# A three-row matmul given all 128 rows through a masked copy, and a store moved to ScalarE's queue

## The chip, the core and the metric

The kernel runs on one core of a Trainium2 chip. The metric is the device time of one execution in microseconds (us); lower is better. Three runs of the kernel before took 2999.73, 3000.49 and 3001.02 us, so its median is 3000.49 us.

## What is computed

Three layers stand behind each other; `x` is 4 batches of 3072 samples by 256.

```
X = fft over 256 of fft over 3072 of x; keep the real part
h = relu(X @ w_in); u, v = halves of h (512 each)
v_n = (v - mean) / sqrt(var + 1e-6)              per sample
v_s = w_spatial (3072x3072) @ v_n + b_spatial
y = (u * v_s) @ w_out
out = (sigmoid(y @ w_gate) * (y @ w_val)) @ w_out2
```

All is in float32; a product is three matmuls of rounded parts (high times high, high times low, low times high), which the kernel calls `mm3`.

## The kernel before

**Stage 1 (about 72 to 362 us)** does the Fourier transform and the first product, for four batches b = 0 to 3. In a batch the outputs come in four *units* (3, 2, 0, 1 in that order), each of 7 or 8 *blocks*: `v_block(m)` makes 128 samples by 512 columns of v, `u_block(fb)` 128 columns of u by 384 samples. A block first runs `mm3` and then one matmul of its own, line 585 in a v block and line 617 in a u block. That one adds the sample at half the rate in the model dimension (index 128 of 256), which the 128 other rows can't hold. It contracts three rows only: `nt` holds, for each unit, three rows of each batch at partitions 32b to 32b+2, zeros elsewhere being of no meaning to it, and `own = slice(32 * b, 32 * b + 3)` picks the batch. ScalarE then copies the sum to `ev` or `eu` (lines 592, 619). Two blocks later comes the block's second half (`second`: `mm3` again, then ScalarE's copy or ReLU at lines 599 and 625 and VectorE's mirror at line 577), and one block later its `rest` (a ReLU on ScalarE, line 605, statistics on VectorE, line 607). A list of steps, one a block, says which other work is written between blocks: folds of the next batch's input (GpSimd, lines 353 to 371), transforms (`fft`, TensorE, the tile `psf`), the taking of transforms into parts `ph`, `pl` (lines 420, 421), normalisation (`ln1` to `norms`, lines 638 to 660) and stores. Every engine runs its instructions in the order in which they are written.

The transforms of units 0 and 1 come out of one pair of sums: ScalarE copies the first half-sum to `even` (line 854), and VectorE makes the other unit's values from it into `value` (line 859). For the last batch the two transforms start at steps 10 and 11 of its 29 (`END0`).

**Stage 2 (about 362 to 1885 us)** is the product with `w_spatial`, by a scheme of seven products in place of eight over 2x2 blocks. It has 42 *leaves* (2 pairs of batches, 7 products, 3 column ranges), each of six steps `kp` of 24 matmuls of 128x512 into four PSUM banks. Operands are loaded five steps ahead by SyncE's queue into 7 staging tiles `st` (line 735), added (line 744, GpSimd for v, VectorE for w), rounded by ScalarE (line 748) and their rest taken by VectorE (line 751). During the next leaf, VectorE takes the four banks (lines 966 to 985), and in the leaves that complete an output also the low parts `gl` (line 993); then two halves of `second` multiply with `w_out` (12 matmuls each), ScalarE copies each half to `x2` (line 1032), and after the other half SyncE's queue stores `x2` (line 1034). There are 24 such stores.

**Stage 3 (about 1885 to 2995 us)** is the last layer, and the change does not touch it.

Of the kernel before, what the change touches and what calls it, by code (L numbers as in the profile page):

```python
# [9 lines left out]
F32 = mybir.dt.float32  # L10
F32R = mybir.dt.float32r
# [3 lines left out]
AF = mybir.ActivationFunctionType  # L15
ALU = mybir.AluOpType
# [3 lines left out]
B, S, D = 4, 3072, 256  # L20
# [4 lines left out]
P = 128  # L25
H = 384
R3 = H + 2
# [105 lines left out]


def _masks():
    m = np.zeros((P, 4), np.float32)
    for b in range(B):
        m[32 * b + 2, 0] = -1.0
        m[32 * b + 1, 1] = -1.0
    m[64:68, 2] = -1.0  # L140
    return m
# [96 lines left out]
def tile_kernel(ctx: ExitStack, tc: tile.TileContext, t: dict, out: bass.AP):  # L238
# [10 lines left out]
    def f(ap):  # L249
        return ap.bitcast(F32)  # L250
# [63 lines left out]
    ps_f = pool(ps0, "ps_f", 2, space=PSUM)  # L314
    ps_w = pool(ps0, "ps_w", 6, space=PSUM)

    masks = keep.tile([P, 4], F32, name="masks")
    gc = [keep.tile([P, 2, DFF], F32R, name=f"g{n}") for n in "hl"]
    g3 = keep.tile([P, DFF], F32R, name="g3")
    nts = [keep.tile([P, R3 if unit == 3 else H], F32R, name=f"nt{unit}") for unit in range(4)]  # L320
# [225 lines left out]
    def take_nyquist(ps, n, unit):  # L546
        nc.scalar.copy(nts[unit], ps[:, :n])
        nc.vector.scalar_tensor_tensor(
            out=nts[unit], in0=f(nts[unit]), scalar=masks[:, 0:1], in1=ps[:, :n], op0=ALU.mult, op1=ALU.add
        )  # L550

    for unit in (3, 2):
        take_nyquist(*fft(fold_n, B, unit, 0), unit)
    s0.close()
    stp = pool(r0, "stp", 2, "right")
    vp = pool(r0, "vp", 13, "right")
# [2 lines left out]
    def unit_blocks(pq, b, unit):  # L559

        (ph, pl), (qh, ql) = pq

        queue = nc.gpsimd if b == B - 1 and unit < 2 else nc.sync
        nt = nts[unit]
        vsl = slice(DH, DFF)

        own = slice(32 * b, 32 * b + 3)
        nb = 7 if unit == 3 else 6
        tiles = {}
        stats = stp.tile([P, 7, 6], F32, name="stats")  # L570
        mv = stp.tile([P, 7, 2], F32, name="mv")
        ve, sd, y, nm = (stp.tile([P, 7], F32, name=n) for n in ("ve", "sd", "y", "nm"))

        def mirror(to, part, ps):
            nc.vector.scalar_tensor_tensor(out=to, in0=part, scalar=2.0, in1=ps, op0=ALU.mult, op1=ALU.subtract)

        def v_block(m):

            w0 = m * P if m < 3 else R3 - P
            win = slice(w0, w0 + P)
            ps = ps_w.tile([P, 512], F32, tag="pa", name="psv")
            mm3(ps, (ph[:, win], pl[:, win]), (gc[0][:, 0, vsl], gc[1][:, 0, vsl]), True, False)
            nc.tensor.matmul(out=ps, lhsT=nt[own, win], rhs=g3[own, vsl], start=False, stop=True)  # L585
            if m == 3:
                tv = vp.tile([P, DH], F32, tag="tv", name="tv")
                nc.scalar.activation(tv, ps, AF.Relu)
                tiles[6] = tv
                return lambda: lambda: nc.vector.bn_stats(stats[:, 6, :], tv)  # L590
            ev = stp.tile([P, DH], F32, tag="e", name="ev", bufs=4)
            nc.scalar.copy(ev, ps)

            def second():
                weights = (gc[0][:, 1, vsl], gc[1][:, 1, vsl])
                mm3(ps, (qh[:, win], ql[:, win]), weights, False, True, skip_group_check=True)
                for sg in range(2):
                    tiles[sg * 3 + m] = vp.tile([P, DH], F32, tag="tv", name="tv")
                nc.scalar.activation(tiles[m], ps, AF.Relu)
                mirror(tiles[3 + m], ev, ps)  # L600
                return rest

            def rest():
                tv = tiles[3 + m]
                nc.scalar.activation(tv, tv, AF.Relu)
                for sg in range(2):
                    nc.vector.bn_stats(stats[:, sg * 3 + m, :], tiles[sg * 3 + m])

            return second

        def u_block(fb):

            fsl = slice(fb * P, fb * P + P)
            n = R3 if unit == 3 else H
            ps = ps_w.tile([P, 512], F32, tag="pa", name="psu")
            mm3(ps[:, :n], (gc[0][:, 0, fsl], gc[1][:, 0, fsl]), (ph[:, :n], pl[:, :n]), True, False)
            nc.tensor.matmul(out=ps[:, :n], lhsT=g3[own, fsl], rhs=nt[own, :n], start=False, stop=True)
            eu = stp.tile([P, R3], F32, tag="e", name="eu", bufs=4)
            nc.scalar.copy(eu[:, :n], ps[:, :n])

            def second():
                weights = (gc[0][:, 1, fsl], gc[1][:, 1, fsl])
                mm3(ps[:, :H], weights, (qh[:, :H], ql[:, :H]), False, True, skip_group_check=True)
                tu = up.tile([P, 2, H], F32, tag="tu", name="tu")
                nc.scalar.copy(tu[:, 0, :], ps[:, :H])
                mirror(tu[:, 1, :], eu[:, :H], ps[:, :H])
                if unit == 3:
                    nc.vector.tensor_copy(tu[:, 1, 0:1], eu[:, H : H + 1])
                at = u_d[b][:, fb, unit * 2 * H : unit * 2 * H + 2 * H]
                return lambda: queue.dma_start(at, tu.rearrange("p a k -> p (a k)"))  # L630

            return second

        a = slice(0, nb)

        def ln1():
            for i in range(nb):
                nc.vector.bn_aggr(mv[:, i, :], stats[:, i, :])
            nc.vector.tensor_scalar(out=ve[:, a], in0=mv[:, a, 1], scalar1=1e-6, scalar2=None, op0=ALU.add)

        def root():
            nc.scalar.activation(sd[:, a], ve[:, a], AF.Sqrt)

        def ln2():
            nc.vector.reciprocal(y[:, a], sd[:, a])

            nc.vector.tensor_tensor(out=sd[:, a], in0=y[:, a], in1=y[:, a], op=ALU.mult)
            nc.vector.tensor_tensor(out=sd[:, a], in0=sd[:, a], in1=ve[:, a], op=ALU.mult)
            nc.vector.tensor_scalar(out=sd[:, a], in0=sd[:, a], scalar1=-0.5, scalar2=1.5, op0=ALU.mult, op1=ALU.add)
            nc.vector.tensor_tensor(out=y[:, a], in0=y[:, a], in1=sd[:, a], op=ALU.mult)  # L650
            nc.vector.scalar_tensor_tensor(out=nm[:, a], in0=mv[:, a, 0], scalar=-1.0, in1=y[:, a], op0=ALU.mult, op1=ALU.mult)

        def norm(i):
            tv = tiles[i]
            if NORM_ON[i] != "a":
                engines[NORM_ON[i]].tensor_scalar(
                    out=tv, in0=tv, scalar1=y[:, i : i + 1], scalar2=nm[:, i : i + 1], op0=ALU.mult, op1=ALU.add
                )
            else:
                nc.scalar.activation(tv, tv, AF.Identity, scale=y[:, i : i + 1], bias=nm[:, i : i + 1])  # L660

        def store(i):
            tv = tiles[i]
            if i == 6:
                q = H - (R3 - P)
                queue.dma_start(v_d[b][0:1, unit * 6 + 3, :], tv[q : q + 1, :])
            elif unit == 3 and i == 3:

                for rows in (slice(16, P), slice(1, 16)):
                    queue.dma_start(v_d[b][rows, unit * 6 + i, :], tv[rows, :])  # L670
            else:
                queue.dma_start(v_d[b][:, unit * 6 + i, :], tv)

        def norms(i):
            for k in (i, i + 3):
                norm(k)
            for k in (i, i + 3):
                store(k)

        def last_norm():  # L680
            norm(6)
            store(6)

        blocks = []
        for i in range(4):
            if i < nb - 3:
                blocks.append(lambda i=i: v_block(i))
            blocks.append(lambda i=i: u_block(i))
        after = [root, ln2] + [lambda i=i: norms(i) for i in range(3)] + ([last_norm] if nb == 7 else [])
        return blocks, [ln1] + after  # L690
# [97 lines left out]


    FOLDS, SPLITS, SPLIT_ON = (-3, 1, 4, 8, 13, 13), (17, 19, 23), "ppp"  # L790
    AT3, AT2, AT0, END0 = (26, 28), (2, 6), (11, 13), (10, 11)
    FIRST, NEXT = 100, (103, 104, 106, 106, 113, 115, 115, 115)
    LAG, NORM_ON, NYQ = 2, "avvvvva", 2
    engines = {"v": nc.vector, "p": nc.gpsimd}
# [44 lines left out]
    def transform(at, b, unit, q, to, also):  # L839
# [15 lines left out]

        def second():
            ps = fft(parts_of[b], b, unit, q, 1, found["ps"][0])[0]
            other = stp.tile([P, H], F32, tag="value", name="value", bufs=1)
            nc.vector.scalar_tensor_tensor(
                out=other, in0=found["even"], scalar=2.0, in1=ps[:, :H], op0=ALU.mult, op1=ALU.subtract  # L860
            )
            found["other"] = (other, H)

        if unit == 0:
# [156 lines left out]
    def second(leaf, o, bank, side):  # L1021
# [9 lines left out]
            side["x2"] = gp.tile([P, 2, 512], F32, tag="x2", name="x2", bufs=1)  # L1031
        nc.scalar.copy(side["x2"][:, o, :], ps)
        if o == 1:
            nc.sync.dma_start(x2_d[(2 * p + mem) * 6 + 3 * th + c], side["x2"])

# [318 lines left out]
```

## Time and profile before

| | us |
|---|---|
| median of three runs | 3000.49 |
| profiled execution, its own time | 3004.6 |
| its span (first to last instruction) | 3002.8 |
| TensorE busy | 2926.9 (97%) |
| VectorE busy | 2093.5 (70%) |
| ScalarE busy | 1315.3 (44%) |
| GpSimd busy | 403.8 (13%) |

PE in the rows is TensorE's matmuls, PEld its weight loads, DVE VectorE, ACT ScalarE, POOL GpSimd, SP SyncE; a "q" behind a name is the engine's sequencer. Matmuls overlap and the ends shown are modelled, so what a matmul takes is read from one start to the next. The mean granted clock of TensorE over the span was 0.982 of full speed.

### The profile page before, as it was taken

To read this page: it belongs to the slowest core of one execution; us is meant where nothing else is said; L and a number is where in the kernel's file an instruction comes from. 1 tells how busy PE (TensorE), PEld (TensorE's weight loads), DVE (VectorE), ACT (ScalarE), POOL (GpSimd) and SP (SyncE) were. 2 spreads that over 40 slices of the span, in tenths; PEclk is the share of its full clock that TensorE was granted. 3 is DMA by queue.
4 is the path that set the end of the run, shared out by engine and by line. 5 is a ranking of instruction groups with operands and counts; after the bars stand their busy time and mean duration, and the time that the engine had idled before them with its cause. 6 is when DMAs were issued, how large, how long until landed. Compare 5 with 4: busy or idle time off the path is not lost.

```text
span 3002.8 us, 34040 instructions
## 1 busy us (share of the span) xinstructions
PE 2926.9 (97%) x12550; PEld 2366.8 (79%) x12550; DVE 2093.5 (70%) x2908; ACT 1315.3 (44%) x2101; POOL 403.8 (13%) x408
## 2 busy tenths in 40 slices
PE   3999999999999999999999999999999999999999
PEld 2777788788878788878887878888888888888887
DVE  8788886867764766667767475876666666666665
ACT  3666532323332232332223232665555555555654
POOL 5774112122110101121102010000000000000000
PEclk8999899999999999999999999999999999999999
DMA  6465786778864667666867475210000000000000
GB/s 227 172 222 204 274 303 208 255 248 295 285 228 145 234 247 261 228 232 237 298 229 244 154 259 185 88 41 29 18 11 29 29 28 29 8 22 29 29 15 14
DMA packets 149656, 472.28 MB, mean 157 GB/s; under 512 B 16624, under 2 KB 18160, under 8 KB 149104
## 3 DMA queue, kind: packets, MB, share of 16 engines
q1 hardware_dynamic: 147168, 455.28, 43.3%
q0 software_dynamic: 2320, 14.82, 1.3%
q8 instruction: 98, 1.61, 0.2%
q14 instruction: 70, 0.57, 0.1%
HBM read 387.46 MB, written 82.58 MB: 157 GB/s over the span
## 4 chain that ended last, share of the span: by engine, by line
PE 89%; DVE 8%; issue 2%; ACT 1%; DMA 0%; DVEq 0%; ACTq 0%; SPq 0%
PE bank L260 27%; PE bank L261 27%; PE bank L259 27%; DVE gl L993 1%; PE psu L259 1%; PE psv L259 1%; DVE vl L751 1%; PE psv L261 1%; PE psv L260 1%; DVE st L744 1%; PE psf L259 1%; PE psv L585 1%; PE psf L260 1%; PE psf L261 1%; PE psu L260 1%
## 5 line engine op out<-in xcount | busy, mean ns | idle before, releaser
L260 PE MATMUL bank<-wl,vh 128*128 128x512 f32 x2016 | 788.8, 391 | 0.0
L259 PE MATMUL bank<-wh,vh 128*128 128x512 f32 x2016 | 788.3, 391 | 0.0
L261 PE MATMUL bank<-wh,vl 128*128 128x512 f32 x2016 | 788.3, 391 | 0.0
L751 DVE TENSOR_TENSOR wl<-st,wh 128x1024 fp32r<-128x1024 f32 x252 | 333.4, 1323 | 388.0 <-ACT wh L748 381.6
L748 ACT CAST wh<-st 128x1024 fp32r<-128x1024 f32 x252 | 265.3, 1053 | 627.1 <-PE bank L261 307.0
L260 PEld LDWEIGHTS bank<-wl,vh 128*128 128x128 f32 x2016 | 380.8, 189 | 80.7
L259 PEld LDWEIGHTS bank<-wh,vh 128*128 128x128 f32 x2016 | 380.7, 189 | 80.2
L261 PEld LDWEIGHTS bank<-wh,vl 128*128 128x128 f32 x2016 | 380.7, 189 | 79.9
L1239 DVE TENSOR_TENSOR t<-t,bank 128x512 f32<-128x512 f32 x144 | 99.1, 688 | 250.3 <-PE bank L261 250.2
L744 DVE TENSOR_TENSOR st<-st 128x1024 f32<-128x1024 f32 x180 | 225.1, 1251 | 66.6 <-DMA st<-in_wt 66.5
L744 POOL TENSOR_TENSOR st<-st 128x1024 f32<-128x1024 f32 x60 | 160.7, 2678 | 805.5 <-DMA st<-v_d 365.1
L260 PE MATMUL bank<-x,wgh 128*128 128x512 f32 x673 | 265.9, 395 | 0.0
L261 PE MATMUL bank<-x,wgl 128*128 128x512 f32 x673 | 265.5, 395 | 0.0
L259 PE MATMUL bank<-x,wgh 128*128 128x512 f32 x673 | 264.0, 392 | 0.1
L1260 DVE TENSOR_TENSOR gl<-s,gh 128x512 fp32r<-128x512 f32 x288 | 199.4, 693 | 57.3 <-ACT gh L1258 44.5
L261 PE MATMUL bank<-gh,wv 128*128 128x512 f32 x576 | 227.6, 395 | 0.0
L259 PE MATMUL bank<-gh,wv 128*128 128x512 f32 x576 | 226.8, 394 | 0.8 <-ACT gh L1253 0.8
L260 PE MATMUL bank<-gl,wv 128*128 128x512 f32 x576 | 225.8, 392 | 0.2 <-DVE gl L1260 0.2
L1230 ACT ACTIVATE s<-s 128x512 f32<-128x512 f32 x144 | 91.0, 632 | 149.1 <-DVE s L1229 149.1
L259 PEld LDWEIGHTS bank<-x,wgh 128*128 128x128 f32 x673 | 126.4, 188 | 30.9 <-DVE s L1229 0.6
L260 PEld LDWEIGHTS bank<-x,wgh 128*128 128x128 f32 x673 | 126.3, 188 | 30.6
L261 PEld LDWEIGHTS bank<-x,wgl 128*128 128x128 f32 x673 | 126.2, 188 | 28.6
(232 smaller groups left out, 4625.8 us busy)
## 6 DMA issues: line engine op xcount, KB each, us to landing
st<-in_wt SPq DMA_DIRECT2D x432, 512.0 KB, 5.7
st<-v_d SPq DMA_DIRECT2D x144, 512.0 KB, 5.3
u<-u_d SPq DMA_DIRECT2D x96, 256.0 KB, 5.7
u_d<-tu SPq DMA_DIRECT2D x56, 384.0 KB, 2.9
v_d<-tv SPq DMA_DIRECT2D x80, 256.0 KB, 2.3
xt<-in_xh SPq DMA_DIRECT2D x24, 512.0 KB, 4.8
x_d<-x SPq DMA_DIRECT2D x24, 512.0 KB, 3.0
raw<-x_d SPq DMA_DIRECT2D x24, 512.0 KB, 4.4
```

The lines of the kernel that those rows point to most:

```text
L259: nc.tensor.matmul(out=ps, lhsT=w[0], rhs=x[0], start=first, stop=False, **kw)
L260: nc.tensor.matmul(out=ps, lhsT=w[0], rhs=x[1], start=False, stop=False, **kw)
L261: nc.tensor.matmul(out=ps, lhsT=w[1], rhs=x[0], start=False, stop=last, **kw)
L585: nc.tensor.matmul(out=ps, lhsT=nt[own, win], rhs=g3[own, vsl], start=False, stop=True)
L744: (nc.gpsimd if kind == "v" else nc.vector).tensor_tensor(out=tiles[0], in0=tiles[0], in1=tiles[1], op=ALU.add if sign > 0 else ALU.subtract)
L748: nc.scalar.copy(hl[0], tiles[0])
L751: lows.append(lambda: nc.vector.tensor_tensor(out=hl[1], in0=tiles[0], in1=f(hl[0]), op=ALU.subtract))
L993: side["low"] = lambda: nc.vector.tensor_tensor(out=gl, in0=g, in1=f(gh), op=ALU.subtract)
L1230: nc.scalar.activation(s1, s1, AF.Sigmoid)
L1239: nc.vector.tensor_tensor(out=g["t2"], in0=g["t2"], in1=g["b"], op=ALU.add)
L1260: nc.vector.tensor_tensor(out=l, in0=s, in1=f(h), op=ALU.subtract)
```

## The change

`masks` gets one column more for each batch: 1.0 in that batch's three rows and 0.0 elsewhere. At the start of every unit ScalarE multiplies all of `nts[unit]` with the batch's column into a new tile `nt`, of which there is one buffer for all 16 units, and the two matmuls take all 128 rows of `nt` and of `g3`. To make room, `value` goes away and VectorE writes over `even`; since `even` has one buffer, the last batch's second transform starts a step later. Apart from this, the stores of `x2` are issued by ScalarE.

```
-    m = np.zeros((P, 4), np.float32)
+    m = np.zeros((P, 3 + B), np.float32)
     for b in range(B):
+        m[32 * b : 32 * b + 3, 3 + b] = 1.0
...
-        nt = nts[unit]
-        own = slice(32 * b, 32 * b + 3)
+        nt = stp.tile([P, R3], F32R, tag="nt", name="nt", bufs=1)
+        nt = nt[:, : R3 if unit == 3 else H]
+        nc.scalar.activation(nt, f(nts[unit]), AF.Identity, scale=masks[:, 3 + b : 4 + b])
...
-            nc.tensor.matmul(out=ps, lhsT=nt[own, win], rhs=g3[own, vsl], start=False, stop=True)
+            nc.tensor.matmul(out=ps, lhsT=nt[:, win], rhs=g3[:, vsl], start=False, stop=True)
...
-            nc.tensor.matmul(out=ps[:, :n], lhsT=g3[own, fsl], rhs=nt[own, :n], start=False, stop=True)
+            nc.tensor.matmul(out=ps[:, :n], lhsT=g3[:, fsl], rhs=nt[:, :n], start=False, stop=True)
...
-    AT3, AT2, AT0, END0 = (26, 28), (2, 6), (11, 13), (10, 11)
+    AT3, AT2, AT0, END0 = (26, 28), (2, 6), (11, 13), (10, 12)
...
-            other = stp.tile([P, H], F32, tag="value", name="value", bufs=1)
-            nc.vector.scalar_tensor_tensor(
-                out=other, in0=found["even"], scalar=2.0, in1=ps[:, :H], op0=ALU.mult, op1=ALU.subtract
-            )
+            other = found["even"]
+            nc.vector.scalar_tensor_tensor(out=other, in0=other, scalar=2.0, in1=ps[:, :H], op0=ALU.mult, op1=ALU.subtract)
...
-            nc.sync.dma_start(x2_d[(2 * p + mem) * 6 + 3 * th + c], side["x2"])
+            nc.scalar.dma_start(x2_d[(2 * p + mem) * 6 + 3 * th + c], side["x2"])
```

ScalarE's instructions at the start of batch 0's unit 0, before the change (`ph<-psf` and `ph<-value` take the transforms of units 0 and 1, `ev` is the copy of the new unit's first block):

```order
L619 COPY eu_907<-psu_902 128x384
L599 ACTIVATE tv_912<-psv_799 128x512
L420 CAST ph_932<-psf_884 128x384
L420 CAST ph_936<-value_926 128x384
L592 COPY ev_951<-psv_946 128x512
L625 COPY tu_956<-psu_839 128x384
L605 ACTIVATE tv_913<-tv_913 128x512
```

and the same place after it:

```order
L622 COPY eu_909<-psu_904 128x384
L602 ACTIVATE tv_914<-psv_802 128x512
L421 CAST ph_933<-psf_886 128x384
L421 CAST ph_937<-even_897 128x384
L570 ACTIVATE nt_941<-nt0_134,masks_130 128x384
L595 COPY ev_954<-psv_949 128x512
L628 COPY tu_959<-psu_841 128x384
L608 ACTIVATE tv_915<-tv_915 128x512
```

The masked copy L570 stands behind everything that ScalarE has to do for the unit before; there are 16 such places. The first block's own matmul, the fourth on TensorE after the unit's start, reads `nt_941`.

SyncE's queue in stage 2, at the first store of `x2`, before:

```order
L735 DMA st_4831<-in_wt 128x1024
L735 DMA st_4833<-v_d0_57 128x1024
L735 DMA st_4835<-v_d1_58 128x1024
L1034 DMA x2_d3_68<-x2_4829 128x1024
L735 DMA st_4884<-in_wt 128x1024
L735 DMA st_4886<-v_d0_57 128x1024
L735 DMA st_4888<-v_d1_58 128x1024
```

and ScalarE's instructions at that place after the change:

```order
L1033 COPY x2_4852<-bank_4839 128x512
L751 CAST wh_4860<-st_4760 128x1024
L1033 COPY x2_4852<-bank_4888 128x512
L1035 DMA x2_d3_68<-x2_4852 128x1024
L751 CAST wh_4913<-st_4798 128x1024
L751 CAST vh_4918<-st_4800 128x1024
L992 CAST gh_4950<-g_4946 128x512
```

The store stands now between ScalarE's second copy to `x2` and its rounding of the next operands, and SyncE's queue goes from the loads before it straight to those behind it.

## Rows read from the trace of the kernel before

**Rows 1.** Windows: stretch; engine busy us (instructions); granted clock; DMA share; GB/s

```profile
72.50:362.00 289.50, 280.83 (x1097) 205.44 (x1097) 238.07 (x541) 187.50 (x374) 150.28 (x227) 0.90 0.59 212
```

**Rows 2.** Waits of PE over the whole span: us, times, longest

```profile
PE bank L260 <- DVE gl L993: 13.0, 6, 2.4
PE psu L259 <- ACT eu L619: 8.7, 6, 2.8
```

**Rows 3.** Windows, sums: 103.2-127.2, 174.5-197.4, 250-270.4, 322-345; then the rest of 72.5-362

```profile
sum 90.30, PE 81.65 PEld 57.12 DVE 87.04 ACT 62.44 POOL 55.91; mean PE 20.41 PEld 14.28 DVE 21.76 ACT 15.61 POOL 13.98
...
sum 199.20, PE 199.18 PEld 148.31 DVE 151.03 ACT 125.06 POOL 94.38; mean PE 39.84 PEld 29.66 DVE 30.21 ACT 25.01 POOL 18.88
```

**Rows 4.** Lines 585 and 617: count, duration ns least/median/most, starts

```profile
L585 PE MATMUL psv<-g,nt x52: 489/496/791, 72.5 to 353.8; 3*128 3x512 f32 x52
...
L617 PE MATMUL psu<-nt,g x64: 432/438/684, 73.6 to 359.9; 3*128 3x384 f32 x48, 3*128 3x386 f32 x16
```

**Rows 5.** Timeline of PE near 161 us: start us, us, instruction

```profile
160.49 0.34 PE L261 MATMUL psf<-c,fl 128*128 128x384 f32 x1
160.66 0.34 PE L413 MATMUL psf<-spc,sps 128*128 128x384 f32 x1
160.84 0.34 PE L259 MATMUL psu<-ph,gh 128*128 128x386 f32 x1
...
161.19 0.34 PE L261 MATMUL psu<-ph,gl 128*128 128x386 f32 x1
161.46 0.43 PE L617 MATMUL psu<-nt,g 3*128 3x386 f32 x1
161.83 0.44 PE L259 MATMUL psu<-ph,gh 128*128 128x384 f32 x1
162.11 0.34 PE L260 MATMUL psu<-pl,gh 128*128 128x384 f32 x1
```

**Rows 6.** Timeline of PE near 206 us

```profile
205.17 0.63 PE L260 MATMUL psv<-gl,ph 128*128 128x512 f32 x1
205.59 0.63 PE L261 MATMUL psv<-gh,pl 128*128 128x512 f32 x1
206.15 0.79 PE L585 MATMUL psv<-g,nt 3*128 3x512 f32 x1
206.87 0.80 PE L259 MATMUL psv<-gh,ph 128*128 128x512 f32 x1
207.47 0.63 PE L260 MATMUL psv<-gl,ph 128*128 128x512 f32 x1
```

**Rows 7.** Timeline, PE and ACT, at the start of batch 0's unit 0

```profile
111.05 0.49 PE L585 MATMUL psv<-g,nt 3*128 3x512 f32 x1
...
112.74 0.51 ACT L420 CAST ph<-value 128x384 fp32r<-128x384 f32 x1
```

**Rows 8.** Timeline, PE and ACT, at the start of batch 1's unit 1

```profile
194.29 0.49 PE L585 MATMUL psv<-g,nt 3*128 3x512 f32 x1
...
197.21 0.60 ACT L599 ACTIVATE tv<-psv 128x512 f32<-128x512 f32 x1
197.70 0.58 ACT L592 COPY ev<-psv 128x512 f32<-128x512 f32 x1
```

**Rows 9.** Waits in stage 2: SyncE's queue (364-1800 us), ScalarE (400-1800 us)

```profile
SPq L1034 <- ACT x L1032: 309.7, 20, 22.8
...
ACT x L1032 <- PE bank L261: 242.0, 40, 7.1
```

**Rows 10.** Timeline, DVE and PE, at the first of PE's six stops in stage 2

```profile
559.69 3.43 DVE L751 TENSOR_TENSOR vl<-st,vh 128x1024 fp32r<-128x1024 f32 x1
...
564.91 0.50 PE L260 MATMUL bank<-gl,woh 128*128 128x512 f32 x1 [2.03 <-DVE gl L993]
```

**Rows 11.** Windows: the ten microseconds behind that stop

```profile
565.00:575.00 10.00, 10.00 (x37) 8.01 (x38) 9.41 (x8) 2.59 (x3) 2.37 (x1) 0.83 0.94 323
```

**Rows 12.** Line 1034: time of the issue on SyncE's queue, ns least/median/most

```profile
L1034 SPq DMA_DIRECT2D x_d<-x x24: 319/323/327, 534.0 to 1898.4; - x24
```

More of the change, by code (lines that the diff above doesn't have):

```diff
@@ L315, in tile_kernel @@
     ps_w = pool(ps0, "ps_w", 6, space=PSUM)
-    masks = keep.tile([P, 4], F32, name="masks")
+    masks = keep.tile([P, 3 + B], F32, name="masks")
     gc = [keep.tile([P, 2, DFF], F32R, name=f"g{n}") for n in "hl"]
```

## The prediction

> **What bounds the kernel now.** I read the busy shares first: TensorE has 97%, so time can only come from TensorE's stops, its clock, or matmuls that take longer than they need. PE's waits over the whole span [rows 2] are the stops of interest: 8.7 us on `eu` in stage 1, and 13.0 us in six stops on `gl` in stage 2. Then the windows: stage 1 [rows 1] takes 289.5 us; PE is busy in 280.8 of it, but at a mean granted clock of 0.90, so 0.10 x 289.5 x 2 = 58 us of it run at 1.2 in place of 2.4 GHz. DVE is busy in 238.1 of the 289.5. The chain of waits splits the stage in two kinds of stretches [rows 3]. In four of them, 90.3 us together, it runs through DVE, which is 87.0 / 90.3 = 96% busy: there a faster TensorE buys nothing. In the rest, 199.2 us, PE is busy throughout and DVE in 151.0 (76%).
>
> Last, the timeline of PE. A matmul over all 128 rows starts 0.17 us after the one before at 384 columns. Around line 617 the three steps from L261 to L260 take 162.11 - 161.19 = 0.92 us in place of 3 x 0.175 = 0.525 [rows 5]: 0.40 too much, spread over the step before the three-row matmul, the step behind it, and one more. At half clock [rows 6] the same three steps take 207.47 - 205.59 = 1.88 in place of 3 x 0.425: 0.60 too much. There are 52 + 64 = 116 such matmuls [rows 4], 13 of them at half clock (those near 0.8 or 0.68 us). What stands for the matmul after the change is L413 [rows 5], which adds a zero-padded operand over 128 rows in the same way: 0.17 us before it and 0.18 behind it, no excess.
>
> **The change part by part.**
>
> *The 116 matmuls.* 42 of them start in the stretches bound by DVE and bring nothing; 74 are left, 13 at half clock: 61 x 0.40 + 13 x 0.60 = 32.2 us off. DVE sets the limit: at its 96%, 151.0 us of work need 157 us, so those 199.2 us can't lose more than 42.
>
> [...]
>
> *The masked copy.* 16 copies of 128x384 on ACT, nearest row 0.51 us [rows 7]: 8.2 us on an engine that is busy in 187.5 of 289.5, hidden as work. What isn't hidden is the new wait: ACT runs in order, so the copy stands behind what ACT has to do for the old unit, and TensorE stops at the new unit's fourth matmul with all that is queued behind it, the second halves of the old unit's blocks too. In the trace the copy would end late by the end of the ACT instruction before its place, plus 0.4 (ACT's next result comes 0.4 to 0.5 behind the last one), minus the start of the three-row matmul. Batch 0's unit 0: 113.25 + 0.4 - 111.05 = 2.6 us [rows 7]. Batch 1's unit 1: 197.81 + 0.4 - 194.29 = 3.9 us [rows 8]. Over the 16 starts: 0.3 for each unit 3, 0.8 to 1.4 for unit 2, 0.8 to 2.6 for unit 0, 3.9 to 6.1 for unit 1, sum 32.7 us. The starts of units 3 and 2 lie where PE is the bound: 5.0 us lost in full. Those of units 0 and 1 lie in or at DVE's stretches, where PE is only ahead and DVE has work in hand; there I charge what it takes to get the first result through again, three matmuls (0.5) and ACT's copy (0.5): 8 x 1.0 = 8 us. Bounds for the wait: 5 (nothing beyond units 3 and 2) and 32.7.
>
> *The clock.* It fell four times in the stage, each time behind a stop of PE of 1 to 3 us, and stayed at 1.2 GHz for 14.5 us on the mean (58 / 4) although PE issued without a gap; in stage 2 each of the six stops, about as long, was followed by only some 3.4 us at half clock (0.83 over ten microseconds) [rows 11]. The difference that I see is the three-row matmul in every fourth place. If the clock comes back as in stage 2, (58 - 8 - 4 x 3.4) / 2 = 18 us more are won; if each of the 8 longer stops is followed by the 14.5 us that the four had, 8 x 14.5 - 58 = 58 us more at half clock cost 29. I take 6 won: four falls of half the length give 14, of which DVE's load leaves less than half.
>
> *The stores of `x2`.* SyncE's queue waits 309.7 us for them in 20 waits, up to 22.8 us each [rows 9], and no load behind them goes out meanwhile; ACT itself waits 242.0 us for PE in the same copies, so the preparation of operands stands still anyhow and only the loads come earlier. PE's six stops come about 30 us behind such a wait, when DVE catches up: DVE's `vl` there takes 3.43 us [rows 10] because GpSimd's late add holds it up, and `gl` stands behind it in order. With loads out up to 20 us earlier, one of these adds moves into the idle time, which is worth about the 2.03 us of the stop. All six gone: 13.0 + 6 x 1.7 (3.4 us at half clock) = 23.2 us won. Against it ACT issues the stores, 24 x 0.32 = 7.8 us [rows 12], just ahead of a `wh` for which DVE waits. Bounds -23 and +8; I take 8 won, as I can't tell whether the order on ACT or the loads decide.
>
> [...]
>
> *The rest.* `even` written in place and the last batch's transform a block later are nothing: the copy to `even` now waits for VectorE's and ScalarE's readers of a block earlier, and the unit that needs the transform starts two blocks later; bounds -1 and +1.
>
> *Sum.* Stage 1: -32.2 + 5 + 8 - 6 = -25; stage 2: -8; together -33. The profiled execution took 3004.6 us, 4.1 above the median of 3000.5; 3004.6 - 33 = 2971.6 for it, and 2967 as a median.
>
> **The rivals.**
>
> *The bound moves to DVE at once.* DVE's small operations already stretch to 1 or 2 us where GpSimd works beside them, GpSimd's 150 us of folds [rows 1] fall into a shorter time, and the stops at unit starts take the lead that PE had. Then the four cycles come down from 72 to some 70 us, stage 1 gains 10, stage 2 half of its 8: 2986. For it: 96% in DVE's stretches. Against: 48 us without DVE work in the rest.
>
> *Both uncertain terms come out well.* The clock stays up, and all six stops go: -42 (DVE's limit) - 23 = -65, 2936; half of that surplus, 2950, is likelier. For it: stage 2's short falls, and that the same stop recurs at the same place six times, so that one cause would remove all.
>
> *Slower: the stops throw the clock.* Mechanism: TensorE stops 32.7 us at unit starts where it stopped 8.7 before (+24), each of the eight long ones is followed by 14.5 us at half clock (+29), and the drains bring 32.2. Sum +21 in stage 1; with stage 2 as forecast +13: 3013. It decides once the time at half clock goes from 58 beyond some 90 us. For it: four stops of 1 to 3 us were enough before. Against: they kept the clock down only while three-row matmuls ran, and PE's lead at units 0 and 1 was idle waiting, not work.
>
> *The excess is not due to the three rows.* If a matmul that ends a sum's first half costs this anyway, only the new wait is left: +24 - 8 = +16, 3016. L413 in rows 5 ends a sum without any excess, which speaks against it. [...]
>
> **How the numbers follow.** Forecast 0.54, its own range 2955 to 2980; DVE bounds at once 0.18 (2980 to 2996); both terms well 0.20 (2936 to 2955); clock thrown 0.06; not the rows 0.02. The two ends of 8 in 10 leave out a tenth each: 2943 below (half of the third case), 2990 above (the slower cases and a few hundredths of DVE's). A measurement of this kernel tells no difference within 0.2%, 6 us. Faster by more: 0.54 + 0.20 + 0.16 = 0.90; within: 0.03, from DVE's case; slower: 0.07, from the last two cases with a margin on the wait.
>
> **What would show it.** The two lines' matmuls a steady 0.17 us (384 columns) and in proportion 0.23 (512) from their neighbours at full clock; 16 ACT instructions of about 0.5 us that write `nt`; in PE's waits a new row for `nt` of 10 to 30 us and none of `eu`; DVE busy in over 90% of a stage 1 that is 20 to 30 us shorter; fewer than 58 us at half clock; no store in SyncE's waits. Wrong would be: the excess still there around the matmuls (then the rows are not its cause), a mean clock below 0.85 in stage 1, a stage 1 shorter by less than 10 us, or six stops on `gl` as long as before (then the loads were not their cause).

## The result, and the profile after

The changed kernel takes 2974.25 us (median of four runs, 2973.02 to 2976.37); the kernel before, run beside it, 3000.11 us. The ratio is 0.9912, with a 95% interval of 0.9897 to 0.9927: 26 us faster, where 33 were forecast, and inside the forecast's own range.

The first row is the window of stage 1 after the change, from the first matmul on `psv` to the first on `bank`, with the columns of [rows 1]; the second is stage 2, to the first matmul of stage 3.

```profile
70.30:344.50 274.20, 231.24 (x1106) 205.91 (x1106) 233.61 (x541) 196.32 (x392) 150.05 (x227) 0.94 0.62 224
...
344.50:1856.60 1512.10, 1505.43 (x6602) 1240.58 (x6602) 1016.09 (x1124) 451.55 (x529) 209.28 (x122) 1.00 0.70 241
```

The same two windows of the kernel before, between the same marks, are:

```profile
71.70:363.90 292.20, 283.53 (x1106) 207.72 (x1106) 239.24 (x543) 188.57 (x376) 151.36 (x229) 0.90 0.59 212
...
363.90:1889.00 1525.10, 1512.12 (x6602) 1245.34 (x6601) 1039.36 (x1123) 450.98 (x529) 211.35 (x120) 0.99 0.68 238
```

Stage 1 is 18.0 us shorter and stage 2 13.0. Together that is 31, more than the 26 of the medians, since the profiled execution of the kernel before was one of its longer ones (3004.6 us). In stage 1 PE's time fell by 283.53 - 231.24 = 52.3 us, and its stops rose from 8.7 to 274.20 - 231.24 = 43.0. Where the clock falls, the granted share is 0.50 (0.50 from 200 to 210 us before, 1.00 from 400 to 500). The time at half clock, (1 - granted clock) x length x 2, went from 58 to 33 us, so in this pair of profiles some 12 of the 52 are the clock's. VectorE was busy in 233.61 / 274.20 = 85% of stage 1.

PE's waits of the whole span after the change (us, times, longest) answer to [rows 2]:

```profile
PE psv L588 <- ACT nt L570: 34.3, 16, 6.3
PE bank L261 <- DVE gl L994: 6.7, 6, 2.3
PE psu L260 <- ACT eu L622: 4.9, 2, 3.2
...
PE psf L260 <- ACT even L857: 3.2, 3, 1.6
```

The large new row is `nt`, one wait for each of the 16 units: 1.5 us at the four units 3, 5.8 at units 2, 6.7 at units 0 and 20.3 at units 1. A small new row is `even`: a transform's matmuls wait for ScalarE's copy to `even`, and that copy waits until VectorE has read the old `even` (2.20 us for VectorE's `pl`, line 422, at the copy of 104.60 us). The wait on `gl` in stage 2 was 13.0 us, and the six stops are still there, half as long (6.7). Next are the two lines with the wide matmuls and the masked copy, which answer to [rows 4], then PE's timeline around one of them, which answers to [rows 5]:

```profile
L588 PE MATMUL psv<-g,nt x52: 389/397/797, 71.5 to 337.9; 128*128 128x512 f32 x52
...
L620 PE MATMUL psu<-nt,g x64: 331/337/525, 72.4 to 340.6; 128*128 128x384 f32 x48, 128*128 128x386 f32 x16
...
L570 ACT ACTIVATE nt<-nt,masks x16: 598/614/625, 70.9 to 328.8; 128x384 fp32r<-128x384 f32 x12, 128x386 fp32r<-128x386 f32 x4
```

```profile
159.86 0.34 PE L262 MATMUL psu<-ph,gl 128*128 128x384 f32 x1
160.04 0.33 PE L620 MATMUL psu<-nt,g 128*128 128x384 f32 x1
160.21 0.34 PE L260 MATMUL psu<-ph,gh 128*128 128x384 f32 x1
160.38 0.33 PE L261 MATMUL psu<-pl,gh 128*128 128x384 f32 x1
```

Three steps now take 160.38 - 159.86 = 0.52 us where they took 0.92: the excess of 0.40 is gone to the last hundredth.

SyncE's queue in stage 2 no longer waits for `x2` [rows 9]. Its waits after the change begin with:

```profile
SPq L738 <- DVE wl L754: 280.6, 150, 8.4
SPq L1005 <- DVE g L986: 263.6, 50, 18.8
```

ScalarE issues the 24 stores in 0.33 us each, as forecast [rows 12]:

```profile
L1035 ACTq DMA_DIRECT2D x_d<-x x24: 326/326/348, 514.2 to 1866.1; - x24
```

### The profile page after: what moved, and what is told of

Read it like the earlier page. It is cut to its first block, busy times and chain, and to the rows that moved or that the text cites. A ratio compares the mean times of both kernels' runs of the same rounds, so it can differ in the third digit from the quotient of the medians.

```text
span 2971.2 us, 34046 instructions
## 1 busy us (share of the span) xinstructions
PE 2867.2 (96%) x12550; PEld 2359.4 (79%) x12550; DVE 2064.7 (69%) x2908; ACT 1323.5 (45%) x2117; POOL 401.2 (14%) x408
## 4 chain that ended last, share of the span: by engine, by line
PE 87%; DVE 8%; ACT 2%; issue 2%; DMA 1%; ACTq 0%; DVEq 0%; SPq 0%
PE bank L261 28%; PE bank L262 28%; PE bank L260 28%; DVE stats L610 1%; DVE gl L994 1%; DVE g L986 1%; ACT wh L751 1%; DVE st L747 1%; DVE tv L580 0%; DVE wl L754 0%; DVE tu L580 0%; DMA v_d<-tv 0%; PE psv L588 0%; DVE tv L659 0%; PE psf L260 0%
## 5 line engine op out<-in xcount | busy, mean ns | idle before, releaser
L754 DVE TENSOR_TENSOR wl<-st,wh 128x1024 fp32r<-128x1024 f32 x252 | 331.4, 1315 | 390.9 <-ACT wh L751 388.9
```

The lines of the kernel that those rows point to most:

```text
L754: lows.append(lambda: nc.vector.tensor_tensor(out=hl[1], in0=tiles[0], in1=f(hl[0]), op=ALU.subtract))
```

## The experiments

Stage times below are cut at the same marks as above. How far a single profile can be trusted shows in kernels whose stage 1 is the same code: 292.2 us before, 288.1 and 288.7 in two experiments that change stage 2 alone; 274.2 after and 277.1 in the first experiment. So a stage 1 carries some 4 us of its own spread. The means are 289.7 and 275.7 us, so 14 is a better figure than 18 for what stage 1 gained, and it goes with the medians: 26 less stage 2's 13. The time at half clock varies as well: 58, 46 and 40 us in the first three kernels, 33 in the other two.

**The two parts apart.** First the wide matmuls with the masked copy alone, then the stores alone.

```
e1_wide_only (from after):   nc.scalar.dma_start(x2_d[...], side["x2"])  ->  nc.sync.dma_start(...)
e2_store_only (from before): nc.sync.dma_start(x2_d[...], side["x2"])  ->  nc.scalar.dma_start(...)
```

> The masked copy and the 128-row matmuls alone; the x2 stores stay on SyncE's queue. If the two parts add up, stage 1 is 18 us shorter as with the whole change (292.2 to 274.2 us from the first psv matmul to the first bank matmul) and stage 2 keeps its six stops on gl with 13 us in all and 20 us at half clock: about 2982 us against 3000, ratio 0.994. Rival: the stops of stage 2 shrank only because stage 1 ended earlier and met the transfers in another phase: then they shrink here too, and the time is that of the whole change, 2974.

> The x2 stores on ScalarE's queue alone, the rest as before. If the blocked queue is what made the six stops, stage 2 is 13 us shorter (stops 13.0 to about 6.7 us, two falls of the clock in place of six) and stage 1 is unchanged: about 2987 us, ratio 0.9957. Rival: the stores have nothing to do with the stops, or ScalarE pays for issuing them: 3000 or up to 8 us more.

They took 2985.33 us (ratio 0.9947, 0.9932 to 0.9962) and 2986.64 us (0.9952, 0.9937 to 0.9967). 0.0053 + 0.0048 = 0.0101 against 0.0088 together: the two parts add within their intervals, each about half of the gain. The waits on `gl`, first of e1_wide_only and then of e2_store_only, went with the stores, so the rival that a shorter stage 1 had shortened them is out:

```profile
PE bank L261 <- DVE gl L994: 13.5, 6, 2.9
```

```profile
PE bank L260 <- DVE gl L993: 5.9, 6, 2.3
```

**The wait without the gain.** The masked copy stays, the two matmuls take three rows of it as before, and the stores are on SyncE's queue.

```
(from e1_wide_only)
+        own = slice(32 * b, 32 * b + 3)
-  lhsT=nt[:, win], rhs=g3[:, vsl]           +  lhsT=nt[own, win], rhs=g3[own, vsl]
-  lhsT=g3[:, fsl], rhs=nt[:, :n]            +  lhsT=g3[own, fsl], rhs=nt[own, :n]
```

> The masked copy stays, and with it TensorE's wait at each unit's start, but the two matmuls contract their batch's three rows again; the stores stay on SyncE's queue. Theory that most of the wait is absorbed (it only takes PE's lead away where VectorE is the bound): 8 to 16 us slower than before, about 3012, with about 30 us of waits for nt in PE's list. Rival, every us of the wait is paid: 25 to 33 us slower, about 3028. Under both the three steps around each such matmul are 0.40 us too long again.

It took 3052.95 us (3044.74 to 3060.06), ratio 1.0172 (1.0146 to 1.0198): far slower than either theory. Its stage 1:

```profile
71.50:413.20 341.70, 323.79 (x1106) 233.61 (x1105) 239.10 (x543) 200.99 (x392) 149.82 (x229) 0.78 0.50 181
```

The sum of stops is only 341.70 - 323.79 = 17.9 us, 9 more than before. What grew is the time at half clock: 0.22 x 341.7 x 2 = 150 us in place of 58, which is 46 us of PE's time. So the rival "the stops throw the clock" describes what is seen here, dearer than I had priced it (150 us and not 8 x 14.5 = 116), but in these runs only while the matmuls are narrow: with the same copy and wide matmuls (e1_wide_only) the clock spent 33 us low although the stops, 277.10 - 233.05 = 44.1 us, were twice as long.

**Which rows cost.** The masked `nt` is zero outside the batch's three rows, so the matmuls may contract any set of rows that holds these three. (From e1_wide_only, with `own` as shown.)

```
e4_rows99:   own = slice(0, 99)
e5_rows32:   own = slice(32 * b, 32 * b + 32)
e12_rows64:  own = the 64 rows of the half that holds the batch's three
```

> The masked copy stays and the two matmuls contract rows 0 to 98 (the masked nt is zero outside the batch's three); x2 stores on SyncE's queue, as in e1_wide_only. Theory A, the excess comes from a matmul that takes only one quarter of the 128 rows beside full ones: 99 rows reach into all four quarters, so line 621's neighbours stay 0.17 us apart, time at half clock about 31 us in stage 1, 2985 us like e1_wide_only. Theory B, any matmul of fewer than 128 rows costs it: three steps around line 621 take 0.92 us again, half clock about 150 us, near 3050 us like e3_wait_only.

> As e4_rows99, with rows 32b to 32b+31 in place of 99. Theories A and B both: three steps around line 621 take 0.92 us, half clock about 150 us in stage 1, 3050 us. Theory C, it is the three rows (a very short column of work) and not the quarter that costs: no excess, 2985 us. [...]

> As e5_rows32, with the 64 rows of the half in which the batch's three lie. If a matmul costs the excess whenever it leaves out a quarter of the rows: three steps around line 621 take 0.92 us, near 3030 us. If only one that takes a single quarter does: 0.53 us, 2985 us.

One run each: 2983.97 us with 99 rows, 3031.65 with 32, 3022.79 with 64. The line of the u blocks in e4_rows99, e5_rows32 and e12_rows64, in this order:

```profile
L621 PE MATMUL psu<-nt,g x64: 335/342/525, 72.8 to 342.9; 99*128 99x384 f32 x48, 99*128 99x386 f32 x16
```

```profile
L621 PE MATMUL psu<-nt,g x64: 433/438/684, 71.5 to 392.1; 32*128 32x384 f32 x48, 32*128 32x386 f32 x16
```

```profile
L621 PE MATMUL psu<-nt,g x64: 435/439/687, 72.9 to 382.2; 64*128 64x384 f32 x48, 64*128 64x386 f32 x16
```

And PE's timeline around it with 64 rows, then with 99:

```profile
164.56 0.34 PE L262 MATMUL psu<-ph,gl 128*128 128x386 f32 x1
164.84 0.44 PE L621 MATMUL psu<-nt,g 64*128 64x386 f32 x1
165.21 0.44 PE L260 MATMUL psu<-ph,gh 128*128 128x384 f32 x1
165.49 0.33 PE L261 MATMUL psu<-pl,gh 128*128 128x384 f32 x1
```

```profile
159.89 0.34 PE L262 MATMUL psu<-ph,gl 128*128 128x384 f32 x1
160.07 0.34 PE L621 MATMUL psu<-nt,g 99*128 99x384 f32 x1
160.25 0.34 PE L260 MATMUL psu<-ph,gh 128*128 128x384 f32 x1
160.43 0.34 PE L261 MATMUL psu<-pl,gh 128*128 128x384 f32 x1
```

165.49 - 164.56 = 0.93 us for three steps with 64 rows, 0.54 with 99; with 32 rows it is 165.60 - 164.68 = 0.92. With 3, 32 or 64 rows the excess is the same 0.40 us; with 99 it is nil. So the cost doesn't grow as the rows get fewer: it is there up to 64 rows and gone at 99. (Nothing between 64 and 99 was tried, so it stays open whether the count decides or that 99 rows reach into all four quarters.)

The clock differs as well. Stage 1 of e5_rows32 and of e12_rows64, with a granted clock of 0.87 and 0.92:

```profile
69.09:395.57 326.48, 296.64 (x1105) 215.21 (x1105) 237.74 (x541) 199.69 (x392) 148.30 (x227) 0.87 0.52 188
```

```profile
70.47:385.57 315.10, 281.27 (x1105) 204.04 (x1105) 239.45 (x541) 199.18 (x392) 149.14 (x227) 0.92 0.54 195
```

By these, 85 us at half clock with 32 rows and 50 with 64, where three rows had 150 and wide ones 33: with the same copy and about the same excess, the fewer rows the matmul took, the longer the clock stayed low. That is one profile each; the times have the same order (3053, 3032, 3023, 2984). Theories A and B had 150 us and 3050 for 32 rows as for three, so that the clock fares better with more rows was not expected.

**No copy at the unit's start.** The mask is put on `g3`, once a batch, in place of `nt`, once a unit; the stores are on ScalarE's queue as after the change.

```
e7_masked_g3 (from after)
-        nt = stp.tile(...); nc.scalar.activation(nt, f(nts[unit]), AF.Identity, scale=masks[:, 3 + b : 4 + b])
+        nt = nts[unit]
+        if unit == 3 and b < B - 1:
+            nc.scalar.activation(gm, f(g3), AF.Identity, scale=masks[:, 3 + b : 4 + b])
+        if unit == 0 and b == B - 2:
+            nc.scalar.activation(g3, f(g3), AF.Identity, scale=masks[:, 2 + B : 3 + B])
+        gb = gm if b < B - 1 else g3          (gb in place of g3 in both matmuls)
```

> As the whole change, but the mask is put on the weights g3 once a batch in place of nt once a unit (for the last batch in place, early), so three copies can be waited for in place of 16. Theory that VectorE bounds the stretches of units 0 and 1 and the waits there only took PE's lead: waits for the mask fall from 34 us to under 6, and the time by some 8 to 12 us against the whole change, about 2964 (stage 1 about 264 us, VectorE busy in 88 to 90% of it). Rival, every us of the 34 was paid: about 30 us less than the whole change, 2944. Other rival, VectorE bounds all of stage 1 already: no gain, 2974.

It took 2957.93 us, ratio 0.9858 (0.9841 to 0.9875), 16 us better than the change: between the theory's 8 to 12 and the rival's 30. Its stage 1 and PE's longest waits in it:

```profile
70.78:331.03 260.25, 230.55 (x1106) 203.74 (x1106) 233.01 (x542) 188.50 (x380) 149.30 (x227) 0.94 0.66 237
```

```profile
PE psu L260 <- ACT eu L626: 22.9, 8, 5.1
PE bank L261 <- DVE gl L998: 5.4, 6, 1.7
PE psv L592 <- ACT gm L571: 2.7, 3, 0.9
```

The 34.3 us for `nt` are gone, and 274.20 - 260.25 = 14.0 us of them came back as time. The rest turned into waits on `eu`: three of 3.8 to 4.7 us stand in unit 1 of the first three batches, where long waits on `nt` stood before, and one of 5.1 us in the last batch. By the trace that last one has another cause: there is no next batch, and ScalarE stands still for a store of `tv` and then for stage 2's operands.

```profile
304.89 0.60 ACT L606 ACTIVATE tv<-psv 128x512 f32<-128x512 f32 x1 [2.96 <-DMA v_d<-tv]
307.50 1.04 ACT L755 CAST wh<-st 128x1024 fp32r<-128x1024 f32 x1 [2.01 <-DVE st L751]
```

**What holds unit 1.** One more of a unit's six normalisations goes from VectorE to ScalarE.

```
e8_norm_act (from e7_masked_g3):  NORM_ON "avvvvva" -> "avvavva"
```

> e7_masked_g3 with one more of six normalisations a unit on ScalarE in place of VectorE (pattern avvavva for avvvvva). Theory, VectorE (90% busy) bounds stage 1 of e7_masked_g3: VectorE's 233 us fall by 8 to 12, stage 1 by 5 to 8, 2951 us against 2958. Rival, ScalarE's added work delays ev and eu, and TensorE's waits on eu (22.9 us) grow by more: 2958 to 2965 us.

2957.46 us (ratio 0.9854, 0.9837 to 0.9871): no change. Its stage 1:

```profile
70.13:331.72 261.59, 229.11 (x1106) 203.14 (x1105) 223.69 (x527) 197.85 (x395) 149.87 (x229) 0.95 0.66 236
```

VectorE worked 9.3 us less and the stage took 1.3 us longer, which speaks against VectorE's amount of work (90% of e7_masked_g3's stage 1) as the bound. It isn't a proof: ScalarE had 9.4 us more to do, and TensorE's waits on `eu` went from 22.9 to 24.4 us, so a gain can have been taken back there. The timeline of e8_norm_act's stop showed ScalarE's normalisation waiting for `nm`, and VectorE's tiny operations before `nm` beside a long `fl` of GpSimd. Two runs were to move that `fl`:

```
e9_split_dve (from e7_masked_g3), e10_after_split (from after):  SPLIT_ON "ppp" -> "ppv"
```

> e7_masked_g3 with the third of a batch's three low parts fl (line 256, 4.7 us on GpSimd in two pieces) written on VectorE ("ppv" for "ppp"). Theory, the stops of 3.8 to 4.7 us at unit 1 come about because VectorE's tiny statistics operations (128x6) stand still while GpSimd's fl runs, ScalarE's normalisation stands behind them and TensorE's eu behind that: the three stops of batches 0 to 2 (13.2 us) go, VectorE gets 2.4 us of work a batch; stage 1 shorter by 6 to 13 us, 2948 us. Rival, VectorE's busy share (90%) is the bound: 7 us more of work make stage 1 longer, 2958 to 2965 us.

> The kernel after with the same one word changed (third fl on VectorE). Theory, the stops at unit 1 for nt (4.2 to 6.4 us, 20.3 of the 34.3 us) have the same cause, ScalarE's normalisation held by GpSimd's fl, with the masked copy queued behind it: nt's wait falls to 20 us or less, 2964 to 2968 us. Rival, the masked copy would be late there anyway, since ScalarE has the old unit's copies to do: nt's wait stays over 28 us, 2972 to 2976 us.

2959.28 us (0.9866, 0.9845 to 0.9886) and 2974.43 us (0.9917, 0.9896 to 0.9937): both as their base, with all stops in place (in e10_after_split 34.5 us for `nt`, as its rival had it). The timeline of the stop in e9_split_dve says why; the rows are POOL's, VectorE's, ScalarE's and PE's:

```profile
116.30 0.18 DVE L652 RECIPROCAL y<-sd 128x6 f32<-128x6 f32 x1
116.45 4.68 POOL L256 TENSOR_TENSOR fl<-fo,fh 128x1024 fp32r<-128x1024 f32 x2
116.51 2.35 DVE L654 TENSOR_TENSOR sd<-y 128x6 f32<-128x6 f32 x1
...
118.89 2.26 DVE L655 TENSOR_TENSOR sd<-sd,ve 128x6 f32<-128x6 f32 x1
121.19 0.17 DVE L656 TENSOR_SCALAR sd<-sd 128x6 f32<-128x6 f32 x1
...
121.80 0.81 ACT L667 ACTIVATE tv<-tv,nm,y 128x512 f32<-128x512 f32 x1 [4.16 <-DVE nm L658]
...
122.51 0.46 ACT L626 COPY eu<-psu 128x384 f32<-128x384 f32 x1
...
123.03 0.69 PE L260 MATMUL psu<-ph,gh 128*128 128x384 f32 x1 [4.75 <-ACT eu L626]
```

Two `fl` run back to back from 116.45 to 121.13, the first for half of that, to 118.79; VectorE's two 128x6 operations end at 118.86 and 121.15. Over the stage the median of the first is 0.17 us:

```profile
L654 DVE TENSOR_TENSOR sd<-y x15: 165/167/2348, 99.9 to 327.8; 128x6 f32<-128x6 f32 x11, 128x7 f32<-128x7 f32 x4
```

But these `fl` are the first and second low part of the batch, late behind GpSimd's folds. The expectation took the two for one; the edit moved the third, a single one of 2.4 us on GpSimd, which runs on VectorE at 128.7 us and was never in the way. So the chain `fl` - `nm` - normalisation - `eu` - TensorE is read from the trace and was not put to the test; the edit that would test it, the first two low parts on VectorE, was not run. The time of 2959 us lies in the rival's range too, but VectorE's work in stage 1 rose by 2.9 us only, from 233.0 to 235.9.

What makes the two operations last so long beside GpSimd was not shown. Not every small one does; in the midst of a later pair of `fl` VectorE's reciprocal took its usual 0.18 us:

```profile
245.61 4.72 POOL L256 TENSOR_TENSOR fl<-fo,fh 128x1024 fp32r<-128x1024 f32 x2
...
246.31 0.18 DVE L652 RECIPROCAL y<-sd 128x6 f32<-128x6 f32 x1
```

The kernel before has such a long operation at the stop's place too, and its 2.26 us count as VectorE's work:

```profile
122.89 2.26 DVE L647 TENSOR_TENSOR sd<-y 128x6 f32<-128x6 f32 x1
```

In the kernel after, the same chain is a part of the stop for `nt` at unit 1 of batch 0, and the instructions that ScalarE has before the copy are the rest:

```profile
121.31 0.81 ACT L663 ACTIVATE tv<-tv,nm,y 128x512 f32<-128x512 f32 x1 [1.90 <-DVE nm L654]
...
122.88 0.61 ACT L570 ACTIVATE nt<-nt,masks 128x384 fp32r<-128x384 f32 x1
...
123.55 0.50 PE L588 MATMUL psv<-g,nt 128*128 128x512 f32 x1 [4.16 <-ACT nt L570]
```

**Which way the stores helped.** In the kernel before, the stores stay on SyncE's queue, but each is issued behind the next leaf's loads of step 3, when `x2` has long been ready.

```
e6b_late_store (from before)
-            nc.sync.dma_start(x2_d[...], side["x2"])
+            late.append((x2_d[...], side["x2"]))      (issued on nc.sync in the next leaf:)
             advance(6 * n + kp + LEAD, 2)
+            if kp == 3:
+                store_late()
```

> The kernel before, with each x2 store issued on SyncE's queue as before but behind the next leaf's loads of step 3, so that it holds up no load. Theory, the loads held behind the waiting store were what made GpSimd's adds late and TensorE stop on gl: stops on gl from 13 to about 6 us, 2987 us as e2_store_only. Rival, what helped was the store's place on ScalarE, or freeing x2 at another time: 13 us of stops stay, 3000 us.

2979.6 us, ratio 0.9934 (0.9915 to 0.9953). Its stage 2, and PE's wait on `gl`, which was [rows 2]'s 13.0 us:

```profile
359.40:1861.90 1502.50, 1502.08 (x6602) 1238.76 (x6602) 1019.77 (x1123) 450.18 (x529) 203.15 (x120) 1.00 0.71 242
```

```profile
PE bank L260 <- DVE gl L993: 0.3, 1, 0.3
```

The six stops are gone but for 0.3 us, PE is busy for 1502.08 of 1502.50 us, and the granted clock is 1.00. Stage 2 is 22.6 us shorter than before, and 9.4 shorter than in e2_store_only (1511.9, stops of 5.9 us), more than the theory gave; the medians of the two kernels differ by 7.0 us, and their intervals overlap. The stops themselves fall in groups by the place of the store: 11.0 to 13.5 us in the six kernels that have it on SyncE's queue ahead of loads, 5.4 to 6.7 in the six that have it on ScalarE's, 0.3 here. The first store goes out 170.1 us into stage 2 before, 170.2 in e2_store_only and 196.4 in e6b_late_store. So the same moment on another queue and a later one on the same queue both shortened the stops; what the two share is that no load stands behind a waiting store (among the long waits of SyncE's queue in stage 2 none is for `x2` in either), and that was the cause, not the time at which `x2` comes free. On ScalarE's queue, ahead of a rounding for which VectorE waits (388.9 us in 143 waits in the kernel after), the stops stay in part; whether the 0.33 us of issue or the earlier moment does that was not separated.

**Both together.** Masked `g3`, the third low part on VectorE, and the late stores on SyncE's queue.

```
e11_best: e9_split_dve with the edit of e6b_late_store in place of nc.scalar.dma_start(x2_d[...])
```

> e9_split_dve with the x2 stores as in e6b_late_store (SyncE's queue, behind the next leaf's loads of step 3) in place of ScalarE's queue. Theory, stage 2 takes 1502.5 us as there and not 1509.7: 7 us less than e9_split_dve, 2941 us. Rival, the two shares don't add: 2948 us.

2953.55 us (2950.11 to 2956.20), ratio 0.9843 (0.9817 to 0.9869), the lowest median of all, but 5.7 us below e9_split_dve where the theory had 7 (its 2941 counted on 2948 for e9_split_dve), with intervals that overlap: stage 2 took 1507.3 us, not 1502.5, and 3.1 us of stops on `gl` stayed:

```profile
PE bank L261 <- DVE gl L998: 3.1, 5, 1.3
```

Why they stay here and not in e6b_late_store, whose stage 2 has the same code, is open.

## Why the prediction was right, and where its sizes were off

The mechanisms of the two parts were right, and the total is better than its terms: stage 1 was forecast 25 us shorter and became 14 to 18 shorter, stage 2 was forecast 8 shorter and became 13. The two errors have opposite signs and cancel in part, which is luck.

- **The 116 matmuls.** Right in mechanism and in the size of one: 0.92 us became 0.52. The cause is wider than "three rows": e5_rows32, e12_rows64 and e4_rows99 show it with 32 and 64 rows and not with 99. The "drains" in the rival with the thrown clock are this excess. Around the three-row matmul a start comes 0.07 and 0.06 us before the end shown for the matmul ahead of it, where full ones overlap by 0.17 [rows 5]; the ends are modelled, and why TensorE starts so late was not shown.
- **The wait for the copy.** Forecast 32.7 us in all, measured 34.3; the copy itself 0.61 us and not 0.51. I charged 13 of it. Taking the copy away (e7_masked_g3) gave 14.0 back, so the charge was about right, but not shown to be so for its reason: the long ones stand at unit 1 (4.16 to 6.35 us each). In the first three batches of e7_masked_g3 TensorE stops there on `eu` without any copy, behind `nm`; in the last the operands of stage 2 hold ScalarE.
- **The step that was mis-sized** is the gain in stage 1 ahead of that charge: I had 32.2 for the matmuls and 6 for the clock, 38 in all; with the copy's wait out, e7_masked_g3 has 292.2 - 260.25 = 32, or 29 against the mean of 289.7. I had TensorE's gain lost in the 90.3 us bound by VectorE [rows 3] and nowhere else. But stops on `eu` of 3.8 to 4.7 us, at unit 1 of the first three batches, stand in e7_masked_g3, and where such a stop stands what TensorE saves before it is lost; how much of the missing 6 to 9 us that is was not measured. Nor was VectorE's 96% all work: an operation of 0.17 us that lasts 2.26 beside GpSimd is in it.
- **The clock.** Fewer than 58 us at half clock: 33. But kernels with the same stage 1 as before had 40 and 46, so the gain is 4 to 12 us and 6 was not clearly too little. That three-row matmuls held it down was a guess from stage 2's short falls; e3_wait_only shows it with 150 us, against 33 in e1_wide_only, which differs in these matmuls alone. The three-row matmuls are not in every fourth place, as I put it, but 116 of the stage's 1106 matmuls. What the trace shows of "1.2 in place of 2.4 GHz" is a granted share of 0.50 in place of 1.00, and the steps of 512 columns in stage 2 before: six in 569.13 - 566.57 = 2.56 us, 0.427 each, in place of 22 in 560.18 - 555.19 = 4.99 us, 0.227 each.
- **The stores.** Forecast 8, measured 13.0 (e2_store_only: 13.2). The upper bound, 23.2 for all six stops with their half-clock time, was met within 0.6 us by e6b_late_store's one profile. So the cause named first, loads held by a queue's head, was right, and the part against it, the store among ScalarE's work, is worth up to 9.4 us of it. As to VectorE's `vl` of 3.43 us [rows 10], GpSimd's add ran beside it from 558.97 to 562.04, and the `vl` at 571.52 with no add beside it took 1.21; that the add holds it up is my reading of this.
- **The rest.** `even` written in place was put at nothing, within 1 us. The trace has three new stops for it, 3.2 us together, and none in the kernel before; what they cost in time was not measured.
- **Signs that did not come.** VectorE was to be busy in over 90% of stage 1 and was in 85%; stage 1 was to be 20 to 30 us shorter; `nt` was to wait 10 to 30 us and `eu` not at all, and they waited 34.3 and 4.9. So the kernel after is not bound by VectorE's work to the extent that the limit of 42 us supposed.
- **The rivals.** "DVE bounds at once" forecast 10 us for stage 1 and had part of the reason: it named VectorE's small operations that stretch beside GpSimd, and these stand ahead of the stops at unit 1 of the first three batches. That VectorE's amount of work is the bound, e8_norm_act and e9_split_dve speak against: 9.3 us less and 2.9 more of it left the time as it was. Excess not due to the rows: refuted by the 0.52 us. Clock thrown: not here, but so with narrow matmuls and the copy. Both terms well, 2936 to 2955 and rather 2950: the change as made doesn't get there; its two ideas, each without its new wait, come into that range with 2953.55 (e11_best).

## What to carry to other kernels

A matmul of few rows between full ones cost 0.40 us here beyond its length: look at the steps from one start to the next around it, and widen it with zeros if the zeros can be had off the critical path, best by masking what changes seldom (once a batch, not once a unit). A store that waited at the head of a load queue was here a wait for every load behind it, 309.7 us in stage 2 [rows 9]: issue it late on the same queue before moving it to a busy engine's. Where an engine's small operation on the way to a release takes ten times its usual time (here 2.35 us for 0.17), look at what runs beside it before counting how busy that engine is.

## What was not expected of the hardware

- With 116 narrow matmuls among 1106 and stops at the units' starts, the clock stayed at half of full speed for 150 us (3 rows), 85 (32) and 50 (64) of stage 1; with full ones and longer stops, for 33.
- A matmul of 99 rows cost its neighbours nothing (0.54 us for three steps), one of 64 rows 0.40 us (0.93), as much as one of three (0.92).
- Two 128x6 operations of VectorE took 2.35 and 2.26 us, each to the end of one of GpSimd's 2.3 us pieces; the first one's median over the stage is 0.17 us.
